# The start of a fused convolution and GELU kernel on one core: the place of two weight loads in GpSimd's queue, and the tile shape of three slots

## The chip, the cores and the metric

The kernel runs on one core of one Trainium2 chip. The metric is the device time of one execution in microseconds (us). The kernel before takes 681.17 us, the median of five runs (680.94 to 681.58).

The core's engines work side by side, each with its own instruction queue: PE (TensorE: matmuls, with PEld for its weight loads), DVE (VectorE), ACT (ScalarE), POOL (GpSimd) and SP (SyncE, which issues DMAs only). They meet through semaphores alone. [...]

## What is computed

```
x (8, 4096, 192) f32, weight (8, 7) f32, w_in (192, 2048) f32, w_out (2048, 192) f32
w   = softmax(weight, per head)                # 7 taps for each of 8 heads of 24 channels
a   = causal convolution of x along the sequence, 7 taps, one set of taps per head
h   = a.reshape(32768, 192) @ w_in
out = gelu_exact(h) @ w_out                    # (32768, 192) f32
```

## The kernel before

**Tiling.** The 32768 tokens are two halves of 16384. A block takes the same stretch of both halves: six blocks of 256 tokens per half, then 29 of 512 (`WS`, line 33). The 192 channels are three planes of 64 (`p`). In a tile the lower 64 partitions hold one half of the tokens and the upper 64 the other (`hf`), so that a matmul contracts 64 channels on 64 rows of the array and two or four matmuls work side by side on different parts of it.

**A block's way.** x comes by DMA into `xin`; DVE transposes it into `xT` (`trans`, line 472). From block 2 on DVE does the convolution as seven multiply-and-adds (`conv`, line 497) and leaves the result in `xc`. Blocks 0 and 1 (`PC`, line 34) are convolved on PE instead, to start sooner: `xT` is cast to bf16 (`cast`, line 216: ACT for block 0, POOL for block 1) into `xTb`, PE multiplies it by seven diagonal matrices `dg` (`pconv`, line 664, its matmuls at line 678 on 64x64 tiles), and ACT and DVE copy the sums out of PSUM into `xc` (`conv_out`, line 186, casts at lines 196 and 198). The six tokens ahead of a block (the halo) are set by a memset for block 0 (line 427) and copied by POOL for the later ones (`halo`, line 394).

Then `mm1` (line 699, matmuls at line 734) multiplies `xc` by W_in, slot by slot, into one of two PSUM buffers `hp`; ACT takes a GELU of 1024 columns of each slot into `gT` (line 648). A block of 256 tokens has 8 slots, one of 512 has 16. A slot of PE may start when the GELU two slots before has emptied its buffer (line 703). The second product with W_out follows one block behind: `mm2` (line 765) for the first blocks, `mm2_t` (line 795) for the later ones, its units laid between the slots of the next block. Results go through `osb` to the output.

**The order at the start.** Everything on POOL is one queue (lines 368 to 421): a wait for DVE's memset of `idb` and two affine selects that make the identity masks (line 380, semaphore S_IDN); a wait for the small `weight` (S_WSB, line 389); W_in's first two issues, for columns 0 to 511 of each half (`win_in`, line 372, S_WIN[0]); four loads of block 1's x (line 391, S_XP[0]); W_in's other two issues (S_WIN[1] and S_WIN[2]); `halo(1)`; W_out's four issues (line 412, S_WOUT[0] to [3]); three casts of block 1; four loads of block 2's x (S_XP[1]); `halo(2)` and so on. These DMAs also turn f32 into bf16 where the tile is bf16.

Block 0's x is loaded by SP (two issues behind that of the small weight, line 844) and ACT (two issues, line 586).

DVE begins with three memsets (lines 425 to 427), waits for the small weight, and makes the softmax of the taps and the columns `wcol` (lines 429 to 450); `wnm`, a 32x32 tile of which the softmax fills 8x7, must have been zeroed before line 438. Then come block 0's first transpose, `dg`, the other two transposes, two of block 0's casts, and `dup(0)`: W_in is loaded once, each half of the columns on one half of the partitions, and DVE copies it to the other half (line 459). Then block 1's transposes, `dup(1)`, and six casts of block 1's convolution, which wait for PE.

On PE, block 0's convolution comes first, then slots 0 to 7 of block 0; block 1's convolution stands in four pieces behind slots 3, 4, 5 and 6 (`behind`, line 697). Slot 4 waits for the second part of W_in (line 713), slots 2 and 6 for the copies (line 715). In `mm1` the width `fw` (line 730) says how many columns of W_in one matmul takes:

```python
fw = 64 if M0 < n <= M1 else 128
for fo in range(0, 128, fw):
    ...
        tile_position=(64 * hf, fo),
```

With `fw` 128 a slot of block 0 is 12 matmuls of 64 rows by 128 columns, two side by side; with 64 it is 24 matmuls of 64x64, four side by side. Blocks 0 to 6 use 128, blocks 7 to 34 use 64.

## Time and profile before

| | |
|---|---|
| median of five runs | 681.17 us (680.94 to 681.58) |
| the profiled execution's own time | 681.17 us |
| its span, first to last instruction | 679.4 us |
| PE busy in the span | 673.8 us, 99% |
| DVE, ACT, POOL busy | 527.8, 536.0, 35.4 us |
| granted TensorE clock | 1.000 |
| software ring (q0): packets, data | 2304, 2.36 MB |
| from issue to landing: a W_in issue, a W_out issue (192 KB each) | 4.7, 6.9 us |

A line of the timeline gives the start and the length in us of a run of like instructions, the engine, the line of the kernel, the operation, the tile written and the tiles read, the tile of the array (64*64 or 64*128) for PE, the shapes, the number of instructions, and in brackets how long the engine stood idle before and what ended that. An engine name with q is a sequencer that issues a DMA. "issue" means that the profile shows nothing that the engine waited for. Times count from the start of the span.

### The profile page before, as it was taken

To read this page: it belongs to the slowest core of one execution; us is meant where nothing else is said; L and a number is where in the kernel's file an instruction comes from. 1 tells how busy PE (TensorE), PEld (TensorE's weight loads), DVE (VectorE), ACT (ScalarE), POOL (GpSimd) and SP (SyncE) were. 2 spreads that over 40 slices of the span, in tenths; PEclk is the share of its full clock that TensorE was granted. 3 is DMA by queue.
4 is the path that set the end of the run, shared out by engine and by line. 5 is a ranking of instruction groups with operands and counts; after the bars stand their busy time and mean duration, and the time that the engine had idled before them with its cause. 6 is when DMAs were issued, how large, how long until landed. Compare 5 with 4: busy or idle time off the path is not lost.

```text
span 679.4 us, 26993 instructions
## 1 busy us (share of the span) xinstructions
PE 673.8 (99%) x12571; PEld 407.4 (60%) x12571; DVE 527.8 (78%) x610; ACT 536.0 (79%) x547; POOL 35.4 (5%) x59
## 2 busy tenths in 40 slices
PE   8999999999999999999999999999999999999998
PEld 4999655555555555555555555555555555555557
DVE  6989978977779877789777798777797777887511
ACT  7899977787778777777877777877878777778772
POOL 7010000000000000000000000000000000000000
PEclk9999999999999999999999999999999999999999
DMA  9336224223433134432144432244422344320123
GB/s 161 98 90 136 71 60 95 53 46 94 96 95 81 41 71 95 96 94 59 45 90 96 96 78 49 65 95 96 95 61 46 86 95 96 83 50 13 48 50 95
DMA packets 131584, 53.64 MB, mean 79 GB/s; under 512 B 125328, under 2 KB 131344, under 8 KB 131472
## 3 DMA queue, kind: packets, MB, share of 16 engines
q1 hardware_dynamic: 128048, 48.97, 30.9%
q0 software_dynamic: 2304, 2.36, 2.1%
q8 instruction: 98, 1.61, 1.0%
q10 hardware_dynamic: 1120, 0.59, 0.3%
q14 instruction: 14, 0.11, 0.1%
HBM read 28.31 MB, written 25.17 MB: 79 GB/s over the span
## 4 chain that ended last, share of the span: by engine, by line
PE 98%; DMA 1%; POOL 1%; issue 0%; DVE 0%
PE hp L734 49%; PE ob L795 43%; PE ob L765 5%; DMA win<-in_moe_w_in_dram 1%; PE hp L765 1%; POOL xin L335 0%; POOL win L372 0%; DMA wsb<-in_weight_dram 0%; PE ob L678 0%; DVE osb L291 0%
## 5 line engine op out<-in xcount | busy, mean ns | idle before, releaser
L648 ACT ACTIVATE gT<-hp 128x1024 bf16<-128x1024 f32 x512 | 522.8, 1023 | 129.2 <-PE hp L734 125.8
L734 PE MATMUL hp<-xc,win 64*64 64x512 bf16 (+2 forms) x6048 | 418.6, 366 | 1.2 <-DMA win<-in_moe_w_in_dram 0.6
L795 PE MATMUL ob<-gT,wout 64*64 64x512 bf16 x5376 | 366.3, 376 | 0.0
L523 DVE SCALAR_TENSOR_TENSOR acc<-xT,wcol,acc 128x1024 f32<-128x1024 f32 (+1 forms) x330 | 295.5, 946 | 3.5 <-ACT acc L621 3.5
L734 PEld LDWEIGHTS hp<-xc,win 64*64 64x64 bf16 (+1 forms) x6048 | 187.8, 106 | 135.4 <-ACT gT L648 2.1
L795 PEld LDWEIGHTS ob<-gT,wout 64*64 64x64 bf16 x5376 | 172.3, 118 | 122.8
L322 DVE STREAM_TRANSPOSE osb<-ob 128x512 f32<-128x512 f32 x84 | 74.5, 889 | 128.9 <-PE ob L795 128.9
L495 DVE STREAM_TRANSPOSE xT<-xin 128x1536 f32<-128x1536 f32 (+2 forms) x39 | 75.0, 1930 | 1.1 <-DMA xin<-in_x_dram 1.0
L523 DVE SCALAR_TENSOR_TENSOR xc<-xT,wcol,acc 128x1024 bf16<-128x1024 f32 (+1 forms) x66 | 60.6, 960 | 0.0
L407 POOL COPY xT<-xT 128x18 f32<-128x18 f32 x30 | 22.5, 751 | 512.6 <-DVE xT L495 489.3
L765 PE MATMUL ob<-wout,gT 64*128 64x192 bf16 x896 | 46.8, 243 | 0.0
L765 PEld LDWEIGHTS ob<-wout,gT 64*128 64x128 bf16 x896 | 38.6, 94 | 5.1 <-issue 0.4
L516 DVE TENSOR_SCALAR acc<-xT,wcol 128x512 f32<-128x512 f32 (+2 forms) x60 | 33.7, 604 | 1.1
L293 ACT ACTIVATE osb<-ob 128x192 f32<-128x192 f32 x2 | 0.7, 330 | 7.1 <-PE ob L765 7.1
L765 PE MATMUL hp<-wout,gT 64*128 64x192 bf16 x128 | 5.9, 243 | 0.0
L291 DVE COPY osb<-ob 128x192 f32<-128x192 f32 x2 | 0.7, 358 | 6.1 <-PE ob L765 6.1
L765 PEld LDWEIGHTS hp<-wout,gT 64*128 64x128 bf16 x128 | 5.3, 94 | 0.0
L198 DVE CAST xc<-ob 64x256 bf16<-64x256 f32 (+3 forms) x8 | 2.9, 357 | 3.1 <-PE ob L678 2.9
L621 ACT ACTIVATE acc<-xT,wcol 128x256 f32<-128x256 f32 (+1 forms) x9 | 5.2, 574 | 0.0
L662 PE MATMUL hp<-const-bfloat16-1.0 128*128 128x512 bf16 x11 | 4.2, 564 | 0.8 <-PEq L869 0.8
L278 ACT ACTIVATE osb<-ob 128x384 f32<-128x384 f32 x10 | 4.9, 486 | 0.0
L335 POOL DMA_DIRECT2D xin<-in_x_dram x8 | 4.8, 616 | 0.0
(35 smaller groups left out, 29.9 us busy)
## 6 DMA issues: line engine op xcount, KB each, us to landing
out_dram<-osb SPq DMA_DIRECT2D x124, 192.0 KB, 3.1
xin<-in_x_dram SPq DMA_DIRECT2D x116, 192.0 KB, 4.2
xin<-in_x_dram SPq DMA_DIRECT2D x14, 96.0 KB, 2.4
win<-in_moe_w_in_dram POOLq DMA_DIRECT2D x4, 192.0 KB, 4.7
xin<-in_x_dram POOLq DMA_DIRECT2D x8, 96.0 KB, 4.2
wout<-in_moe_w_out_dram POOLq DMA_DIRECT2D x4, 192.0 KB, 6.9
out_dram<-osb ACTq DMA_DIRECT2D x4, 96.0 KB, 2.0
out_dram<-osb SPq DMA_DIRECT2D x4, 96.0 KB, 2.6
```

The source lines that it names most:

```text
L278: e.activation(out=dst, in_=src, func=AF.Copy).then_inc(S_EVA)
L322: v.transpose(ap(osb[m % 2], j, [[8 * C, 128], [C // 2, TB // 32], [NP, 32]]), bank(ring(m, j)),).then_inc(S_EV)
L335: e.dma_start(ap(xin[n % NX], 32 * q * (TB // 32 * DQ), dst), ap(xt, off, src)).then_inc(sm or S_XIN[n % NX], 16)
L407: g.tensor_copy(dst, src).then_inc(S_HALO)
L495: v.transpose(out, src).then_inc(S_TR)
L516: ins = v.tensor_scalar(a, src, wk, None, ALU.mult)
L523: ins = v.scalar_tensor_tensor(dst, src, wk, a, op0=ALU.mult, op1=ALU.add)
L621: a.activation(out=acc[n % 2][:, p * TB : p * TB + w], in_=ap(xT[n % 2], p * XW + HX, [[NP * XW, 128], [1, w]]), func=AF.Copy, scale=wcol[ ...
L648: a.activation(out=ap(gT[n % 2], i * c * 2 * w, dst), in_=ap(hp[u % 2], 0, src), func=AF.Gelu,).then_inc(S_GELU)
L734: ins = t.matmul(hp[u % 2][fo : fo + fw, o : o + w], ap(win, f1, [[NP * F, 64], [2, fw]]), xc[n % 2][r, p * TB : p * TB + w], start=(p == ...
L765: ins = t.matmul(bb[sub], gT[m % 2][r, c0 : c0 + 128], wout[r, CH[sub][i] * C : (CH[sub][i] + 1) * C], start=(ph == 0 and k == 0), stop=(p ...
L795: ins = t.matmul(bank(ring(m, j), slice(64 * h, 64 * h + 64), w), ap(wout, 64 * hf * NF * C + CH[h][i] * C + j, [[NF * C, 64], [NP, 64]],) ...
```

## The change

Three things are edited. On POOL the wait for the small weight is gone; in its place POOL waits for its own masks, and does the memsets of `wnm` and of block 0's halo, which DVE did. W_out's four issues move from behind `halo(1)` to right behind W_in's. In `mm1`, slots 4, 5 and 6 of block 0 take `fw` = 64. DVE waits for `wnm` on a new semaphore, S_WNM.

```diff
+        S_WNM = sem("S_WNM")
...
-            g.wait_ge(S_WSB, 16)
+            g.wait_ge(S_IDN, 2)
+            g.memset(wnm[:, :], 0.0).then_inc(S_WNM)
+            g.memset(ap(xTb[0], HF, [[NP * XB, 128], [XB, NP], [1, HB]]), 0.0).then_inc(S_HALO)
             win_in(FP[0], FP[1], [S_WIN[0]] * 2)
             load(g, 1, sm=S_XP[0])
             win_in(FP[1], FP[2], S_WIN[1:])
+            for k in range(4):
+                g.dma_start(
+                    ap(wout, 2 * k * C, [[NF * C, 128], [8 * C, 2], [1, 2 * C]]),
+                    ap(woutt, 256 * k * C, [[2 * C, 128], [1024 * C, 2], [1, 2 * C]]),
+                ).then_inc(S_WOUT[k], 16)
...
-            g.wait_ge(S_IDN, 2)
             halo(1)
-            for k in range(4):
-                g.dma_start(
-                    ap(wout, 2 * k * C, [[NF * C, 128], [8 * C, 2], [1, 2 * C]]),
-                    ap(woutt, 256 * k * C, [[2 * C, 128], [1024 * C, 2], [1, 2 * C]]),
-                ).then_inc(S_WOUT[k], 16)
...
             v.memset(idb[:, :], 1.0).then_inc(S_MSET)
-            v.memset(wnm[:, :], 0.0).then_inc(S_MSET)
-            v.memset(ap(xTb[0], HF, [[NP * XB, 128], [XB, NP], [1, HB]]), 0.0).then_inc(S_HALO)
             v.wait_ge(S_WSB, 16)
...
-            v.wait_ge(S_MSET, 2)
+            v.wait_ge(S_WNM, 1)
...
-                        fw = 64 if M0 < n <= M1 else 128
+                        fw = 64 if (n == 0 and 4 <= i <= 6) or M0 < n <= M1 else 128
```

## The prediction

> **What bounds the kernel now.** I read the page's chain that ended last, the same chain in order of time for the first 20 us, the timeline of 8 to 18.5 us, and the DMA queues of the stretch in which the software ring (the queue of POOL's DMAs) starts. From the page:

> ```profile
> PE 98%; DMA 1%; POOL 1%; issue 0%; DVE 0%
> ```

> From 18 us to the last matmul (676.60) PE is busy 658.58 of 658.60 us. So nothing after 18 us can be won by waiting less, and whatever the start gains or loses goes to the end one for one. The chain's first 13 us:

> ```profile
> 0.81 1.33 DMA wsb<-in_weight_dram
> 2.14 0.30 issue
> 2.43 1.38 POOL win L372 x2
> 3.82 2.35 POOL xin L335 x4
> 6.17 0.36 POOL win L372
> 6.54 0.22 issue
> 6.75 5.84 DMA win<-in_moe_w_in_dram
> 12.60 0.14 issue
> 12.73 0.83 PE hp L734 x12
> ```

> POOL holds its first W_in issue until the small weight has landed (2.43); behind it go block 1's four x loads and the second pair of W_in; the last row of that pair lands at 12.60 and releases slot 4 of block 0. The same place in the timeline:

> ```profile
> 9.12 3.89 ACT L648 ACTIVATE gT<-hp 128x1024 bf16<-128x1024 f32 x4 [0.78 <-PE hp L734]
> 11.87 0.52 PE L678 MATMUL ob<-xTb,dg 64*64 64x256 bf16 x12
> 12.73 0.83 PE L734 MATMUL hp<-xc,win 64*128 64x256 bf16 x12 [0.34 <-DMA win<-in_moe_w_in_dram]
> 13.50 0.52 PE L678 MATMUL ob<-xTb,dg 64*64 64x256 bf16 x12
> 13.95 0.83 PE L734 MATMUL hp<-xc,win 64*128 64x256 bf16 x12
> 14.71 0.31 PEld L678 LDWEIGHTS ob<-xTb,dg 64*64 64x64 bf16 x16 [0.21 <-issue]
> 14.71 0.47 PE L678 MATMUL ob<-xTb,dg 64*64 64x256 bf16 x16
> 15.05 2.29 DVE L198 CAST xc<-ob 128x256 bf16<-128x256 f32 x6 [1.74 <-PE ob L678]
> 15.12 0.83 PE L734 MATMUL hp<-xc,win 64*128 64x256 bf16 x12
> 15.88 0.42 PE L678 MATMUL ob<-xTb,dg 64*64 64x128 bf16 x16
> 16.23 1.79 PE L734 MATMUL hp<-xc,win 64*128 64x256 bf16 x24
> ```

> Slots 4, 5, 6, 7 start at 12.73, 13.95, 15.12, 16.23; between them stand block 1's convolution matmuls (L678) on another tile shape. Block 1's first slot (the second half of the last row) starts at 17.07, and its third pair, at 17.40, waits for the last of DVE's six casts (15.05 + 2.29 = 17.34). That chain sets when the steady stretch begins.

> **Part 1, the first W_in issue.** POOL's two masks end at 1.08 + 0.53 = 1.61. Behind them now stand a wait on POOL's own semaphore (0.03 us, by DVE's own from 2.97 to 3.00) and two memsets; POOL's nearest row, L401's 128x18, took 0.113. The issue starts at about 1.85 in place of 2.43, **0.58 earlier** (0.43 to 0.65 with memsets of 0.2 or 0.08 each). The first packet came 1.48 after the issue's start (2.43 to 3.91), so it would come at 3.33. What the ring meets there:

> ```profile
> DMA  9697995996676344443322222111000000044300
> q1 hardware_dynamic: 168, 0.06, 37.3%
> q10 hardware_dynamic: 19, 0.01, 3.4%
> q0 software_dynamic: 3, 0.00, 3.2%
> ```

> This is 3.3 to 4.0 us: 187 rows of block 0's x (SP's and ACT's queues) run out, engine after engine, before the ring starts. The engines are busy 43.9% of 0.7 us, so 0.39 us of each stand idle on average; from 4 to 5 us the ring alone keeps them at 95.8%, and POOL's issues (7.38 the last of W_in) are far ahead of its packets. So the ring's whole stream moves up by the idle time that is filled: 0.40. It is 0 if the engine that finishes x last (3.90) is also the one that lands W_in last, and 0.58 if all of it counts; I take 0.40, the mean of the row. W_in's last landing is then 12.20, and slot 4 starts at 12.33 (0.13 after it, as now). PE is ready for it at 11.87 + 3 x 0.11 = 12.20, ACT's third GELU ends at 9.12 + 2 x 0.96 + 1.02 = 12.06, so both stay just ahead. Slot 4 gains 0.40 (0 to 0.55). Slot 0 gains at most 0.07: it waited 0.29 for W_in (8.25), but the casts that it also needs end at 8.09.

> DVE loses two memsets (0.09 and 0.07) ahead of a wait of 1.09 for the small weight: nothing. They cost 0.16 only if the weight came before 1.07. DVE's new wait S_WNM (needed at 3.19) and PE's for the halo (first convolution, 5.78) are for memsets done by 1.85: covered by 1.3 and 3.9.

> **Part 2, W_out ahead of halo(1).** Four issues of 0.72 (L412, 713 to 748 ns) move from 7.57 to about 6.8; halo(1) moves from 7.42 to about 9.7. Queued behind it are block 1's casts on POOL, which wait for DVE's transposes at 10.40 anyway, and x2's loads behind those (11.89), so neither moves. PE needs halo(1) at 11.87: covered by 1.9, and as late as it comes if not. W_out's own landings (13.76 to 17.16) come earlier with the stream, and PE asks for them from 17.85 on: nothing to win. If x2 came later, DVE's block 2 (last cast 26.76, used by PE from 27.72) would give 0.96 of cover.

> In this trace W_in's two copies on DVE (8.44 to 9.85) lie beside the second and third W_out issue, and all four issues took alike, 713 to 748 ns. [...]

> **Part 3, four 64x64 tiles in slots 4 to 6.** A slot of six pairs streams 6 x 0.11 (pair spacing (0.83 - 0.27)/5); the convolutions behind slots 4, 5, 6 are 3 fours of 256 columns (0.33), one of 256 and three of 128 (0.275), four of 128 (0.22). From slot 4 to 5: 1.22 - 0.66 - 0.33 = 0.23 is left over; 5 to 6: 1.17 - 0.935 = 0.235; 6 to 7: 1.11 - 0.88 = 0.23. The timeline's weight loads say where: the first after each change of shape stands idle 0.20 to 0.21 with nothing to wait for. That is 0.115 a change. With one shape, the changes 4-to-behind, behind-to-5 and 5-to-behind go before DVE's first cast is fed (0.345); three more changes stand ahead of slot 4 or behind that feed and are not on the path. The slots now load 24 weights of 64x64 instead of 12 of 64x128: L678's rows show 107 ns against 94, four side by side under 110 of streaming. Bounds: 0.345 if they hide as L678's do; if a four took the 118 ns that L795's loads take, 12 x 0.008 = 0.10 less.

> Would ACT then bind? Slots would come 0.99, 0.94, 1.0 apart, GELUs need 0.96: just covered, 0.02 lost at most.

> **Sum.** DVE's casts start 0.40 + 0.345 = 0.75 earlier, block 1's third pair at 16.65, and PE streams from there. The profiled execution took 681.17 (span 679.4 and 1.77 around it), the same as the median of the five: 681.17 - 0.75 = **680.4**.

> **Rivals.**
> 1. *The ring's stream hardly moves,* because its slowest engine had no idle time: slot 4 gains 0 to 0.15, and 0.345 comes on top: 680.75. For it: W_in's landings spread from 10.45 to 12.60 over the engines, so one engine decides. A mild form of rival 2 ends here too (680.6 to 681.1).
> 2. *W_in collides with block 0's x: slower than before.* At 3.33 an average engine has 187/16 = 12 x rows left, the last one (done at 3.90) about 27. A W_in row holds an engine 0.15 us (106 in 4 to 5 us on 16 engines), an x row 0.021 (607 in 2.5 to 3.3). Taken in turn, 12 rows end at 5.4 and 27 at 7.9. DVE's first transpose of x (4.61) waits now for its own work, with 0.65 to spare; all of block 0 hangs on it. Slot 4 would be ready at 12.13 + s, with s the delay of that transpose, and the end gain 0.93 - s; from an x landing of 5.5 (s = 0.93) the change loses. With x at 6.3: 681.17 - 0.93 + 1.7 = 681.95. For it: where SP's and ACT's queues overlap (2.5 to 3.3) both move, 339 rows and 268. Against: no stretch here shows the software ring beside them, and if engines share by bytes (2 KB read for a W_in row, 384 B for an x row), 27 x rows need only five W_in rows, 0.75, and x lands at 4.65, when it is needed.
> 3. *The four tiles save no change of shape* (W_in's strided weights behave unlike L678's): 681.17 - 0.40 = 680.75.

> [...]

> **Chances.** Forecast 0.43; rival 1 with the mild collision 0.25; rival 2 0.23; rival 3 0.06; other 0.03. A measurement of this kernel tells about 0.2% (1.36 us) from no change; the largest gain here, 0.93, is less. Faster by more: 0.03. Slower by more needs s above 2.3: 0.09. Within: 0.88. The range holds the forecast's bounds (680.2 to 680.8), rival 1, rival 3 and more than half of rival 2: 680.2 to 682.1.

> **What would show it.** First W_in issue near 1.85 and its packets near 3.33; the first transpose of x still at 4.61 (later: rival 2); W_in's last landing near 12.20 (12.5: rival 1); no idle 0.2 before weight loads between slots 4 and 6 (else rival 3); DVE's six casts from 14.3; block 1's third pair near 16.65; PE without gaps from 18 us on. A new gap there, or a longer stay in slots 0 to 3, would make the prediction wrong.

## The result, and the profile after

The changed kernel takes **682.23 us** (median, 681.65 to 684.55) against 681.24 (680.70 to 681.95) for the kernel before beside it: ratio 1.0017 [1.0012, 1.0022]. It moved to the slow side by about one microsecond, where the forecast was 0.75 to the fast side; 682.23 lies just above the upper end of the range, 682.1.

The profiled execution took 682.4 us, its span is 680.7 (before 681.17 and 679.4), and the clock was 1.000 in both. The page's chain by engine, and its row for the queue that carries instructions:

```profile
PE 98%; ACT 1%; DVE 1%; issue 0%; DMA 0%; ACTq 0%
...
q8 instruction: 99, 1.62, 1.0%
```

POOL and W_in's transfer are no longer in the chain (they had 1% each). Queue q8 moved one packet more (98 packets, 1.61 MB in the kernel before), and PE has 72 instructions more: 12607 matmuls and as many weight loads, against 12571 of each.

**Where the time came in.** The first matmul with W_out starts at 19.10 in place of 17.85, and the last matmul ends at 677.83 in place of 676.58: 1.25 later at both ends. The stretches answer in one row (length, busy us and count of PE, PEld, DVE, ACT and POOL, clock, DMA share, GB/s):

```profile
19.10:677.90 658.80, 658.73 (x12344) 398.45 (x12338) 516.79 (x579) 522.34 (x528) 19.83 (x32) 1.00 0.34 77
```

PE is busy there without a gap, as before. So the whole difference is made ahead of 19.1 us. The chain of the changed kernel in order of time (start, length, what):

```profile
12.68 0.66 PE hp L734 x24
13.34 0.33 PE ob L678 x12
13.67 0.66 PE hp L734 x24
14.32 0.28 PE ob L678 x16
14.60 0.50 PE hp L734 x16
15.10 1.79 issue
16.89 0.44 PE hp L734 x8
17.33 0.02 issue
17.36 1.03 ACT gT L648
```

And the timeline of PE:

```profile
12.16 0.52 PE L678 MATMUL ob<-xTb,dg 64*64 64x256 bf16 x12
12.51 0.82 PE L734 MATMUL hp<-xc,win 64*64 64x256 bf16 x24
13.17 0.50 PE L678 MATMUL ob<-xTb,dg 64*64 64x256 bf16 x12
13.50 0.82 PE L734 MATMUL hp<-xc,win 64*64 64x256 bf16 x24
14.15 0.45 PE L678 MATMUL ob<-xTb,dg 64*64 64x256 bf16 x16
14.47 0.63 PE L734 MATMUL hp<-xc,win 64*64 64x256 bf16 x16
16.89 0.41 PE L734 MATMUL hp<-xc,win 64*64 64x256 bf16 x8 [1.79 <-issue]
17.13 0.40 PE L678 MATMUL ob<-xTb,dg 64*64 64x128 bf16 x16
```

Up to 14.47 the change does what it was to do: slots 4, 5 and 6 start at 12.51, 13.50 and 14.47 (before 12.73, 13.95, 15.12), so PE is 0.65 ahead. Then it stops in the middle of slot 6, after 16 of its 24 matmuls, for 1.79 us. Nothing can change there between one matmul and the next: the operands of the 17th (`xc`, W_in, the PSUM buffer) are those of the slot, and the slot had already begun. The profile says "issue": it shows nothing that PE waited for. The weight loads, which run a little ahead of the matmuls (13.39 against 13.50 in slot 5), stop at the same place and for longer:

```profile
13.39 0.66 PEld L734 LDWEIGHTS hp<-xc,win 64*64 64x64 bf16 x24
...
16.89 0.14 PEld L734 LDWEIGHTS hp<-xc,win 64*64 64x64 bf16 x8 [2.06 <-issue]
```

It looks as if neither queue of PE had an instruction, which is a reading of these two stops. The DMA queues of 14.5 to 15.6 us (packets, MB, share of 16 engines) show what was late:

```profile
q0 software_dynamic: 194, 0.29, 105.6%
q8 instruction: 1, 0.02, 5.5%
```

One packet of 16 KB runs on the instruction queue, from 14.58 to 15.54, among the software ring's packets, and PE goes on 1.35 after its end.

**The theory.** PE's program comes in pieces of 16 KB on q8 (98 packets, 1.61 MB in the kernel before). Number the matmuls and weight loads that the profile records by their start. Between successive such packets, once W_out and block 2's x have left the software ring, lie 244 to 296 of them in the first stretches of before (the packets start at 684, 932, 1188, 1452, 1696, 1992), 256 on the average of the whole run; and 1.61 MB over 25142 instructions is 64 bytes each, so by this count a packet is 256 instructions. Counting back from 684 in such steps, the kernel's first packet would be due near instruction 172, which PE reaches at 9.1 (9.4 in the changed kernel); this is an estimate. It came at 14.40 in before, when PE had done 321. The theory says that PE can't pass its 438th recorded instruction (the 439th in four kernels below) until that packet is in: no profile shows it pass sooner, and in the changed kernel and seven of those below it stopped there, for 0.4 to 2.3 us. Before passed the 438th at 17.06, after the packet; the 36 matmuls and 36 loads of part 3 bring it forward to 14.8, ahead of the packet. *Rivals:* part 3's strided 64x64 weights stop PE by themselves; the early issues (parts 1 and 2) disturb a transfer that PE needs.

### The profile page after: what moved, and what is told of

It reads as the page before. It is cut to its first block, busy times and chain, and to the rows that moved or that the text cites. A ratio compares the mean times of both kernels' runs of the same rounds, so it can differ in the third digit from the quotient of the medians.

```text
span 680.7 us, 27064 instructions
## 1 busy us (share of the span) xinstructions
PE 673.2 (99%) x12607; PEld 407.9 (60%) x12607; DVE 528.0 (78%) x608; ACT 535.9 (79%) x547; POOL 32.8 (5%) x61
## 4 chain that ended last, share of the span: by engine, by line
PE 98%; ACT 1%; DVE 1%; issue 0%; DMA 0%; ACTq 0%
PE hp L734 49%; PE ob L795 43%; PE ob L765 5%; PE hp L765 1%; ACT gT L648 0%; PE ob L678 0%; DMA wsb<-in_weight_dram 0%; DVE xT L495 0%; DVE wcol L447 0%; DVE dg L547 0%; ACT xTb L222 0%; ACT wex L589 0%; ACT xc L197 0%; DVE osb L292 0%; DVE wnm L438 0%
## 5 line engine op out<-in xcount | busy, mean ns | idle before, releaser
L648 ACT ACTIVATE gT<-hp 128x1024 bf16<-128x1024 f32 x512 | 522.7, 1023 | 130.2 <-PE hp L734 126.9
L734 PE MATMUL hp<-xc,win 64*64 64x512 bf16 (+3 forms) x6084 | 418.7, 365 | 2.7 <-issue 1.8
L795 PE MATMUL ob<-gT,wout 64*64 64x512 bf16 x5376 | 366.3, 376 | 0.0
L734 PEld LDWEIGHTS hp<-xc,win 64*64 64x64 bf16 (+1 forms) x6084 | 188.1, 106 | 136.4 <-issue 2.1
L795 PEld LDWEIGHTS ob<-gT,wout 64*64 64x64 bf16 x5376 | 172.3, 118 | 122.8
L415 POOL COPY xT<-xT 128x18 f32<-128x18 f32 x30 | 19.7, 657 | 516.4 <-DVE xT L495 489.9
L678 PE MATMUL ob<-xTb,dg 64*64 64x256 bf16 (+1 forms) x112 | 4.0, 246 | 1.1 <-ACT xTb L222 1.0
```

What stands on the lines that cost most here:

```text
L415: g.tensor_copy(dst, src).then_inc(S_HALO)
L648: a.activation(out=ap(gT[n % 2], i * c * 2 * w, dst), in_=ap(hp[u % 2], 0, src), func=AF.Gelu,).then_inc(S_GELU)
L734: ins = t.matmul(hp[u % 2][fo : fo + fw, o : o + w], ap(win, f1, [[NP * F, 64], [2, fw]]), xc[n % 2][r, p * TB : p * TB + w], start=(p == ...
L795: ins = t.matmul(bank(ring(m, j), slice(64 * h, 64 * h + 64), w), ap(wout, 64 * hf * NF * C + CH[h][i] * C + j, [[NF * C, 64], [NP, 64]],) ...
```

## The experiments

Each kernel ran beside the kernel before on one chip; where the difference is below a microsecond, the place of the stop in the profile tells more than the ratio. A profile shows one execution, which can lie off the median of its kernel: 680.74 against 681.11 in p1, 680.91 against 681.66 in quads_p13, 682.99 against 682.09 in quads_p3, 683.9 against 682.12 in p13.

### The parts alone: p3, p1, p12, p13

p3 keeps only the tile shape:

```diff
-                        fw = 64 if M0 < n <= M1 else 128
+                        fw = 64 if (n == 0 and 4 <= i <= 6) or M0 < n <= M1 else 128
```

> The tile shape alone: slots 4 to 6 of block 0 on four 64x64 tiles, 72 PE instructions more, everything else as before. Refill theory: PE reaches recorded instruction 438 in the middle of slot 6 at about 15.1, where it stands idle until 16.6 to 16.9; 682.0 to 682.4, so all of the loss comes from this part. Rival, the collision: no loss here, the changes of tile shape are saved and it takes 680.7 to 681.0.

Measured: 681.94, ratio 1.0016 [1.0007, 1.0024]: the whole loss, with POOL's order untouched. Its PE timeline stops at the same matmul as the changed kernel's, the 17th of slot 6:

```profile
14.41 0.63 PE L734 MATMUL hp<-xc,win 64*64 64x256 bf16 x16
16.02 0.41 PE L734 MATMUL hp<-xc,win 64*64 64x256 bf16 x8 [0.98 <-issue]
...
18.23 0.82 PE L765 MATMUL ob<-wout,gT 64*128 64x192 bf16 x16
```

The packet ran from 13.68 to 14.64, PE resumed 1.38 after it. The early issues are not needed for the loss.

p1 has only the first edit (W_out behind `halo(1)`, `fw` 128):

```diff
-            g.wait_ge(S_WSB, 16)
+            g.wait_ge(S_IDN, 2)
+            g.memset(wnm[:, :], 0.0).then_inc(S_WNM)
+            g.memset(ap(xTb[0], HF, [[NP * XB, 128], [XB, NP], [1, HB]]), 0.0).then_inc(S_HALO)
```

> The early W_in issue alone (memsets on POOL, no wait for the small weight); W_out and the tile shape as before. Refill theory: PE's program comes in blocks of 256 instructions (16 KB packets of the instruction queue q8), the second refill packet of block 0's time is held up behind the software ring (14.40 to 15.29 before), and PE cannot pass its recorded instruction 438 until some 1.35 us after that packet's end. With no instruction added PE reaches 438 at about 17.1, after the refill is usable (16.7): no idle PE in block 0's slots with 'issue' as its cause, 680.9 to 681.3. Rival, the collision alone (the ring's early start delays the small weight by 0.3 and that is the whole loss): 681.5 to 682.2.

Measured: 681.11 against 681.06, 1.0002 [0.9992, 1.0011]. In its profile W_in's last row lands at 12.08, the first W_out matmul starts at 17.43, 0.42 earlier than before, and the span is 679.0 (before 679.4). The 438th instruction passes at 16.64 without a stop; its packet ended at 14.81. The profile shows part 1's 0.40; the median of the runs doesn't, though the interval would allow it (0.40 is 0.0006).

p12 has both orders on POOL and `fw` 128:

> The early W_in issue and W_out right behind it, tile shape as before. Refill theory: no PE idle by 'issue', slot 4 about 0.2 to 0.3 earlier, the rest as before: 680.8 to 681.2. Rival, the collision: 681.5 to 682.2, as for the early issue alone.

Measured: 681.75, 1.0008 [0.9999, 1.0017]; the packet ran 14.44 to 15.33, the 438th passed at 17.14 without a stop. Nothing is gained or lost beyond the measurement's reach, but the median is above the 680.8 to 681.2 that I expected, and the profile doesn't show part 1's gain either: W_in's last row lands at 12.57 and slot 4 starts at 12.70 (12.08 and 12.32 in p1). p13 is the changed kernel with W_out's issues back behind `halo(1)`:

> The early W_in issue and the four tiles; W_out's issues behind halo(1) as before. Refill theory: PE stops at recorded instruction 438 at about 14.6 until some 1.35 after the refill packet's end. With the early issue alone that packet ended at 14.81, so until about 16.2, which is 0.7 before the changed kernel: 681.4 to 681.9, between the early issue alone and the changed kernel. Rival, that W_out's place does not matter: 682.2.

Measured: 682.12, 1.0022 [1.0011, 1.0032]. The packet ran 14.26 to 15.23, the stop lasted from 14.70 to 16.77, PE's own share of it 1.80. (This execution also lost time behind the stop: its slot 7 starts at 17.34, 0.12 ahead of the changed kernel's, and its span is 682.2 against 680.7, at a mean granted clock of 0.997.) So the order of W_out's issues is not the cause either: with part 3 in, the loss is there with W_out early or late.

### The same tiles at another place: fw012

```diff
-                        fw = 64 if (n == 0 and 4 <= i <= 6) or M0 < n <= M1 else 128
+                        fw = 64 if (n == 0 and i <= 2) or M0 < n <= M1 else 128
```

The POOL part is that of before. Slots 0 to 2 have no convolution piece behind them, so on balance no change of shape is saved (one goes ahead of slot 0, one comes behind slot 2); the same 72 instructions are added, but earlier in the program.

> The kernel before with the four tiles in slots 0 to 2 in place of 4 to 6: the same 72 more PE instructions, but the shape of slots 4 to 6 as before. Refill theory: PE again stops at recorded instruction 438, which now lies in the middle of slot 6, until 16.5 to 16.9: 681.8 to 682.4. Rival, that the shape of slots 4 to 6 itself stalls PE: no idle stretch there, 681.0 to 681.3.

Measured: 681.27, 1.0001 [0.9992, 1.0010]. The stop that I had expected didn't come:

```profile
15.22 0.83 PE L734 MATMUL hp<-xc,win 64*128 64x256 bf16 x12
15.98 0.42 PE L678 MATMUL ob<-xTb,dg 64*64 64x128 bf16 x16
16.33 1.23 PE L734 MATMUL hp<-xc,win 64*128 64x256 bf16 x16
```

The packet ran from 11.22 to 13.06, some three microseconds earlier, and PE passed the 438th instruction at 15.35. The miss corrected the theory: instructions added early also bring forward the place at which the next piece is due (the 184th instruction, close behind that place, starts at 8.77 in place of 10.20), not only the place where PE stops. It also speaks against the first rival: these strided 64x64 weights cost PE no stop.

### Instructions added, shapes untouched: quads_before, and its fellows

Behind the warm-up stand 24 tiny matmuls into a PSUM buffer that is written again later; they are 48 PE instructions and compute nothing that is used. quads_before adds them to the kernel before.

```diff
+            for i in range(6):
+                for hf in range(2):
+                    r = slice(64 * hf, 64 * hf + 64)
+                    for fo in (0, 64):
+                        t.matmul(hp[1][fo:fo + 64, 512 * hf:512 * hf + 64],
+                                 one[r, 0:64], one[r, 0:64], tile_position=(64 * hf, fo))
```

> The kernel before with the same 24 small matmuls: what they do alone. Refill theory: PE did not stop before, so an earlier refill gives nothing: 680.9 to 681.3. If the small matmuls themselves helped (a warmer PE), this run would gain as much as the others.

Measured: 681.63, 1.0009 [1.0000, 1.0018]. Its PE timeline has a stop that before does not have, and no tile shape has changed:

```profile
15.28 0.83 PE L744 MATMUL hp<-xc,win 64*128 64x256 bf16 x12
16.04 0.25 PE L688 MATMUL ob<-xTb,dg 64*64 64x128 bf16 x4
16.66 0.36 PE L688 MATMUL ob<-xTb,dg 64*64 64x128 bf16 x12 [0.37 <-issue]
```

It falls after the 438th recorded instruction again, now within the convolution piece behind slot 6 (L688 is L678 here). The packet ran from 14.29 to 15.26, and PE resumed 1.40 after it. I had expected no stop, because I thought that the added instructions would bring the packet forward as in fw012. This is the run that settles it: with POOL's order and the shapes as before, the count alone makes the stop, and it moves with the count.

quads_p3 adds the same matmuls to p3, quads_after to the changed kernel, quads_p13 to p13.

> The tile shape alone, with the same 24 small matmuls. Refill theory: no stop either (681.94 without the small matmuls); slot 4 waits for W_in as before, the changes of shape are saved: 680.6 to 681.0.

> The changed kernel with 24 small matmuls (64 columns, four 64x64 tiles, 48 PE instructions) behind the warm-up, in the 0.7 us in which PE waits for the first convolution anyway. Refill theory: PE crosses its first block of 256 instructions at about 8.4 in place of 10.2; with a crossing at 8.8 (four tiles in slots 0 to 2) the refill packet started at 11.22. So it starts near 11.3, is usable by about 13.7, and PE is not due at recorded instruction 438 (now behind slot 5) before 14.4: no stop, and the shape and the early W_in give what the prediction counted, 0.7 to 0.9: 680.2 to 680.6. Rival, that the stop belongs to slot 6: 682.2.

> The early W_in issue and the four tiles with the 24 small matmuls, W_out's issues behind halo(1) as before. Refill theory: no stop; if W_out's place costs something of its own, this one is ahead of the changed kernel with the small matmuls, else equal: 680.2 to 680.6.

Measured: quads_p3 682.09, 1.0012 [1.0003, 1.0021]; quads_after 681.80, 1.0013 [1.0004, 1.0022]; quads_p13 681.66, 1.0007 [0.9998, 1.0015]. In quads_p3 the 48 instructions stand ahead of slot 6 and move the stop out of it, into the convolution piece behind slot 5:

```profile
13.54 0.85 PE L744 MATMUL hp<-xc,win 64*64 64x256 bf16 x24
14.19 0.36 PE L688 MATMUL ob<-xTb,dg 64*64 64x256 bf16 x8
16.90 0.31 PE L688 MATMUL ob<-xTb,dg 64*64 64x128 bf16 x8 [2.34 <-issue]
```

The packet ran 14.54 to 15.49 there (resumed 1.41 later); 13.49 to 14.45 in quads_after (stop 14.30 to 15.97, resumed 1.52 later); 12.36 to 13.26 in quads_p13 (stop 14.24 to 14.83, 1.57 later). I had expected no stop in any of the three. The stop's length is the packet's lateness, as the theory has it. What I can't predict is when the packet comes: it differs by two microseconds between kernels in which it is due at almost the same time (their 172nd instruction starts at 7.57 in quads_p3, at 7.84 in quads_p13).

### The ring kept empty: held, held_fw128, held2

If the ring's packets hold the instruction packet back, it must come at once when the ring is empty. held is the changed kernel with W_out's issues behind POOL's casts; block 2's x goes to SP, which issues it once W_in has landed.

```diff
-            load(g, 2, sm=S_XP[1])
+            for k in range(4):
...
+                ).then_inc(S_WOUT[k], 16)
...
+            sp.wait_ge(S_WIN[1], 16)
+            sp.wait_ge(S_WIN[2], 16)
+            load(sp, 2, sm=S_XP[1])
```

> The changed kernel, but W_out's four issues go behind POOL's casts of block 1 (about 12.3), and block 2's x is loaded by SP once all of W_in has landed, so that the software ring holds nothing but W_in when PE asks for its next block of instructions (about 10). Refill theory: the refill packet starts before 12.6 in place of 14.58, is usable by about 14.6, and PE does not stop at recorded instruction 438 (14.85): 680.3 to 680.8. Rival, that the stop has nothing to do with what stands in the ring: it stays at 16.9, 682.2. A later W_out could itself cost 0.3 to 1 in block 1's first slots (its waits would then show there).

Measured: 682.51, 1.0019 [1.0010, 1.0028]. The DMA queues of 10.9 to 12 us:

```profile
DMA  0000900000000000000000000000000000000000
...
q8 instruction: 1, 0.02, 5.4%
```

The packet is alone (11.01 to 11.96), 3.6 earlier than in the changed kernel. It starts as the ring runs out: the last packet of W_in and block 1's x ends at 10.77 (11.01 in held_fw128, 11.62 in held2, where the instruction packet starts at 10.98 and 11.56). That is also 1.8 to 1.9 after PE's 172nd instruction in all three, so whether it waited for the ring or takes that long by itself isn't shown. PE's stop is gone, and its timeline shows the gain and where it went:

```profile
14.11 0.85 PE L733 MATMUL hp<-xc,win 64*64 64x256 bf16 x24
14.79 0.40 PE L677 MATMUL ob<-xTb,dg 64*64 64x128 bf16 x16
15.12 1.96 PE L733 MATMUL hp<-xc,win 64*128 64x256 bf16 x24
16.92 0.49 PE L764 MATMUL ob<-wout,gT 64*128 64x192 bf16 x8
17.84 0.50 PE L764 MATMUL ob<-wout,gT 64*128 64x192 bf16 x8 [0.43 <-DMA wout<-in_moe_w_out_dram]
...
20.75 0.42 PE L764 MATMUL ob<-wout,gT 64*128 64x192 bf16 x6 [1.41 <-DMA wout<-in_moe_w_out_dram]
```

All 24 matmuls of slot 6 run through, and the first W_out matmul starts at 16.92, **0.93 earlier than before**: the gain of parts 1 and 3 is real when PE has its program. But W_out now lands at 16.11 to 20.70, and PE waits 1.84 for it. For PE W_out has to be in the ring early; for the instruction packet, on the theory, late.

held_fw128 is held with `fw` 128; held2 is held with SP waiting for W_out's first part ahead of block 2's x.

> The same with slots 4 to 6 on 64x128 tiles as before: what the held ring is worth without the tile shape. Refill theory: no stop in either, so this one is slower than the one with four tiles by the saved changes of shape, 0.3 to 0.45: 680.7 to 681.2.

> W_out's issues behind POOL's casts as in the run in which the refill started at 11.01, but block 2's x is loaded by SP only when W_out's first issue has landed, so that W_out's rows have the engines alone at first. Refill theory: no stop at 438; W_out's landings move from 16.1, 17.8, 18.8, 20.7 to about 15, 16.5, 17.7, 18.8, so PE's waits for it (1.8 there) shrink to under 0.5: 680.5 to 681.1. If block 2's x then comes too late for DVE, a gap shows before block 2's first slot (26.8) and the gain is lost again.

Measured: held_fw128 681.71, 1.0010 [1.0001, 1.0019]; packet 10.98 to 12.39, one wait of PE for W_out, 0.53. held2 683.19, 1.0031 [1.0019, 1.0042]; packet 11.56 to 12.51, no stop, W_out still not landed until 20.66, and DVE's block 2 too late by 0.75 as its x landed at 21.69. Neither keeps the gain.

### The request brought forward: pad, pad_late, pad_late_p13

fw012 suggested more instructions very early, so that the packet is due before W_out fills the ring. pad puts 56 of the tiny matmuls ahead of the warm-up and cuts that from 11 to 7 large ones; pad_late puts 52 behind the full warm-up (the loop above with `range(13)`); pad_late_p13 does that to p13.

> The changed kernel with 104 more PE instructions in the warm-up: 56 matmuls of 64 columns on four 64x64 tiles and 7 of 512 columns in place of 11 of 512, in less time. Refill theory: PE crosses its first block of 256 some 104 instructions earlier, at about 6.5 in place of 10, so the first refill comes earlier too (before 11.5); PE must then stop, if it does, at recorded instruction 438 = early in slot 5 (13.5) or 256 later, in block 1's second slot (about 18.5), and not in the middle of slot 6. If the second refill is in time: 680.4 to 680.9; if it is held up behind block 2's x: up to 682. Rival, that the place of the stop belongs to slot 6 and its waits: it stays in slot 6, at 682.2.

> The changed kernel with 52 small matmuls (104 PE instructions) behind the warm-up; with 24 of them the refill packet still started at 13.49, with 104 instructions inside the warm-up at 11.33. Theory A, an earlier crossing of the first block (here at 7.4) brings an earlier refill: start near 11.3, usable by 13.7, no stop or one under 0.3 at recorded instruction 438 (now early in slot 5), 680.2 to 680.8. Theory B, the start is set by the rows in the software ring whatever the crossing: 12.4 to 14.6, and PE stops in slot 5 from 13.5 until 15 to 17: 681.5 to 683.

> The same without the move of W_out's issues (they stand behind halo(1)). Theory A: 680.2 to 680.8 as well. Theory B: a stop in slot 5, 681 to 682.5; with W_out 0.2 later in the ring a little earlier than with the move.

Measured: pad 681.35, 1.0007 [0.9998, 1.0015]; pad_late 681.66, 1.0011 [1.0002, 1.0020]; pad_late_p13 681.82, 1.0011 [1.0002, 1.0020]. In pad (packet 11.33 to 12.28) and pad_late (11.01 to 12.06) the stop at the 438th instruction is gone, and something else is late. In pad the convolution of block 0 starts at 5.99 and takes 3.20 (before 5.78 and 2.18), so slot 0 starts at 9.12 in place of 8.25. The trace shows how it is slower: PE runs at half its later pace for the first microseconds of its work. (The granted clock, 1.00 in both kernels as a mean, doesn't tell why: in before the trace's record of it begins at 4.34.) In before the warm-up's matmuls start 0.43 apart up to 4.2 and 0.22 apart at 4.5, and pairs of convolution matmuls 0.11 apart from 5.9 on; in pad the shortened warm-up is 0.43 apart to its end, and pairs stay 0.21 apart until 9.7. That the shorter warm-up is the reason wasn't tried. In pad_late the packet fell among W_in's last rows: they landed at 13.24 in place of 12.35, and slot 4 waited until 13.38. Fifteen of the sixteen DMA engines had landed their share by 12.21; the profile doesn't say which engine ran the packet, so that it was the packet that held up the sixteenth is argued. In pad_late_p13 the packet came at 12.51 to 13.47 and PE stopped from 13.29 to 14.75. No kernel tried beats the kernel before.

## Why the prediction was wrong

*Part 1, first issue of W_in.* Right in its mechanism. The issue stands at 1.78 (said 1.85). In the stretch from 3.2 to 3.4 us the software ring has packets, where the kernel before has none (said 3.33). W_in's last row lands at 12.35 and slot 4 starts at 12.51 (said 12.20 and 12.33; before 12.60 and 12.73). Of the 0.40 forecast for slot 4, 0.22 came in this execution, in which the small weight also landed 0.32 later than before and slot 4 followed the convolution without a wait for W_in; in p1 0.41 came (12.32), in p12 0.03. All within the bounds 0 to 0.55. Rival 1, a gain of 0 to 0.15, fits p12 and neither of the others.

*Rival 2, W_in against block 0's x.* Its mechanism exists but is small: x's last row lands at 4.52 in place of 4.43, and in the profiles of all kernels at 4.37 to 4.87 with the early issue, 4.30 to 4.43 without. The first transpose of x started at 4.61 to 4.70 in eight of the twelve kernels with the early issue, and directly behind x at 4.76, 4.82 and 4.89 in three. The changed kernel's 4.97 came from the late small weight. The rival was to decide from an x landing of 5.5, so x lost 0.09, at most 0.44, where 1.07 was needed; its end, 681.95, was nearly hit, for another reason. Its 5.4 and 7.9 rested on rows that are taken in turn, which was my estimate; for x beside W_in these 0.09 to 0.44 speak against it. For the instruction packet beside the ring the runs don't settle how the two share the engines: with W_out kept out of the ring it came at 11.0 to 11.6, beside W_out mostly at 12.4 to 14.6, but at 11.0 to 11.3 in three kernels.

*Part 2, W_out's issues.* Right for PE's cover, although W_out's last two parts landed later, not earlier (17.09 and 17.72, before 16.60 and 17.16). The run times show no difference by the order itself (p12 beside p1, the changed kernel beside p13; their intervals overlap). The profiles hint at one: with the early issue W_in's last row landed at 11.83 to 12.23 in the four kernels with W_out behind `halo(1)`, and at 12.30 to 12.57 in the three with W_out ahead of it and no instruction packet beside W_in's end, no earlier than the 12.30 to 12.76 of the five kernels without the early issue. So part 2 may take back what part 1 gives; these are single executions, and it wasn't tried by itself. And the step's "nothing to win" named only PE's cover. The 16 DMA engines that W_out's packets use have another customer, PE's program (q8: 1.0% of their time in the whole run, one packet from 14.58 to 15.54 here), which the step left out.

*Part 3, four tiles, the saving.* Right: slots 4, 5 and 6 start 0.99 and 0.97 apart (said 0.99 and 0.94), the idle 0.2 ahead of weight loads between them is gone, and the 24 small loads of slot 5 (0.66 in all) hide under its streaming (0.82). Rival 3 falls. By the start of DVE's casts, 14.47 against 15.05, 0.58 of the 0.75 had been won.

***The step that failed* is part 3's cost of "24 weights of 64x64 instead of 12 of 64x128".** It counted 36 added matmuls and 36 added loads by their streaming and load time alone (bounds 0.345 or 0.10 less) and left out that they are also 72 more places in PE's program, whose next piece was late already. The term's measured size: 1.79 us of PE at 15.10. With 0.65 won by slot 6 and 1.25 lost at the first W_out matmul, the sum is 0.65 + 1.25 = 1.90, the stop and 0.11 of what follows it. The profile of before had the evidence, a q8 packet from 14.40 to 15.29 (in its DMA queues of 14.3 to 15.4 us), and PE past instruction 438 only at 17.06:

```profile
q0 software_dynamic: 277, 0.24, 122.4%
q8 instruction: 1, 0.02, 5.1%
```

```profile
16.22 0.55 PEld L734 LDWEIGHTS hp<-xc,win 64*128 64x128 bf16 x12
17.06 0.12 PEld L734 LDWEIGHTS hp<-xc,win 64*128 64x128 bf16 x4 [0.29 <-ACT gT L648]
```

With the 1.35 after the packet that after shows, PE would have been free to go on from 16.64: 0.4 of cover, which neither term of the sum was allowed to use up, and the sum used 0.75 and the 72 instructions.

"A new gap there, or a longer stay in slots 0 to 3, would make the prediction wrong" pointed to after 18 us; the gap came at 15.1.

*What is shown and what stays open.* Shown, by one profiled execution of each kernel: the count alone makes the stop (quads_before), the stop moves with the count (quads_p3), it ends 1.28 to 1.57 after the packet in all eight kernels that have it, and it goes when the packet comes early (held, pad, pad_late). Open: what sets the moment at which the packet starts while the ring is busy. It was 11.0 to 11.3 in fw012, pad and pad_late, 12.4 to 14.6 in the other kernels with W_out in the ring by then, among them the four kernels with 48 extra instructions, in which it is also due early. Argued, not shown: the spread of single runs (quads_p3 680.45 to 682.99, pad_late 680.84 to 683.40, before 680.70 to 681.95 beside the changed kernel) would fit a packet that is caught in some executions and not in others. A part of it has another source: nine executions, of the changed kernel (3), p3 (1), p13 (3), quads_after (1) and pad_late (1), have a mean granted clock of 0.997 or 0.998 and took 682.67 to 684.55, and no execution of the other kernels, nor of the kernel before beside the experiments, has one below 0.999; why isn't shown.

## What to carry to other kernels

An instruction can cost time by its place in the program as well as by its own length: here 48 instructions whose results nobody used made a stop of 0.37 us (quads_before), 72 one of 1.79. Before doubling the count of matmuls in a short stretch near the start, look in the profile for the instruction queue's packets, when they come, and which instruction the engine has reached by then (here it stopped behind the 438th or 439th). A transfer that shares the DMA engines with PE's program may cost time even if nobody waits for its data: without W_out in the ring the packet came at 11.0 to 11.6, with it mostly at 12.4 to 14.6, but at 11.0 to 11.3 in three kernels, so the runs suggest this and don't show it. Where an engine idles by "issue" between two instructions of one loop, with weight loads and matmuls stopped together, look at that queue first.
